# Taking the reciprocal of the decays' running product on GpSimd as a power of -1, from chunk 4 on

## Chip, cores and metric

The kernel runs on one core of a Trainium2 chip. The metric is the device time of one execution in microseconds (us). Two timed executions of the kernel before gave 775.13 and 778.49 us, median 776.81 us. The profile is of a third execution, which took 782.45 us; its span from first to last instruction is 780.6 us, so 1.85 us lie around the span.

Names: PE is the matrix engine (TensorE), PEld its weight loads, DVE is VectorE, ACT is ScalarE, POOL is GpSimd, and SP is the engine whose queue issues most of the DMAs.

## The reference

Two blocks follow each other. The first is a recurrence over 768 time steps for 4 batches and 8 heads with a 40x40 state each; the second is a two-layer feed-forward block on its 3072x320 output.

```python
# recurrence, state (B, H, D, D), B, H, S, D = 4, 8, 768, 40
for t in range(S):
    y[:, :, t] = np.einsum('bhd,bhde->bhe', rt, state)
    Sa = np.einsum('bhde,bhe->bhd', state, at)
    state_decay = state * wt[:, :, None, :] - np.einsum('bhd,bhe->bhde', Sa, bt)
    state = state_decay + np.einsum('bhd,bhe->bhde', vt, kt)
...
x = attn_out.transpose(0, 2, 1, 3).reshape(B * S, H * D)
h = x @ w_in            # 320 -> 2048
g = h * np.cos(h)
return g @ w_out        # 2048 -> 320
```

The decays `w` lie between 0.85 and 0.95.

## The kernel before

The 768 steps are cut into 24 chunks of 32 steps. A chunk has 128 rows (4 batches by 32 steps), so each of its inputs is a tile of 128 partitions by 320 columns (8 heads by 40). Inside a chunk the recurrence is written as small matrix products. For that the decays are multiplied up along the chunk, and `b` and `k` are divided by this running product while `a` is multiplied by it. The division needs the reciprocal of the product, a tile `rw` of 128x320 for every chunk.

From chunk 4 on the running products come from memory: `ws_scan` multiplies them up for four chunks at once, `ws_store` writes them out to `wd`, and `load` reads them back into `nat_w` (two buffers, one for even chunks and one for odd). For chunks 0 to 3 they come out of PSUM (`wn`), which is not touched by the change.

The order of all work is written out by hand in a string, `PLAN`. Each token stands for one step, and the steps are emitted in this order, so every engine and every DMA queue runs its own instructions strictly in that order. The tokens that matter here, with the lines of the profile:

- `r:c` is `over_w` (L453 to L457): the reciprocal `rw` (L455, DVE), then `bn` = `b` times `rw` on POOL (L456).
- `pw:c` is `p1_w`, for two chunks: transposes of `nat_w` on PE, a copy `wb` on ACT (L442), a small copy `wc` (L444) and a memset of the first columns of `wb` to 1 (L451), both on POOL.
- `pa:c` is `p1_a`: transposes of `nat_a` on PE (tile `aps`), then `aT` = `aps` times `wb` on DVE (L461).
- `pb:c` is `p1_b`: transposes of `bn` on PE (tile `bT`, L411) and copies on ACT. `pn:c` multiplies `bT` and `aT` on PE (tile `nps`); ACT copies the result for the inversion, a chain of small DVE steps (`ip`, `ij`; L545 to L576).
- `kn:c` is `p2_kn`: `k` times `rw` on POOL (L631), and a copy of `v` (L632). `in:c` is `p2_in`: copies of `v` and `r` on POOL (L625). `k:c` and `v:c` transpose them on PE (`kT`, `vT`).
- `z:c` is `ch_z`, the state's step: products on PE (tile `dps`), an addition on DVE (L806), the multiplication of the state tile `qz` by the decays on POOL (L807, four instructions), and the output rows `yt` (addition on DVE L813, multiplication on POOL L818). The next chunk starts with `t:c+1`, transposes of `qz` on PE (tile `sT`, L697).
- `tk:c` stores `yt` to DRAM (`xd`, L828, SP queue), `tb:c` reads it back turned as `xT` (L839, L841). `xT` feeds the feed-forward block: `fa`/`fb` (first layer, tile `ph`), `y` (cosine and product on ACT and DVE), `sd` (second layer, tile `po`).
- `ld:c:w` is `load` (L238) of a chunk's `nat_w`, four DMAs on the SP queue. It may overwrite the buffer only once the reciprocal of chunk c-2 has read it.
- `wf`, `wt`, `wg`, `wm`, `wp` (L313 to L340) fetch and convert the feed-forward weights in the first 160 us, mostly on DVE and ACT. `B` and `K` are matrix products without use that keep PE running in the first 150 us.

The inversion is done for four chunks at once. From about 160 us on the feed-forward block of earlier chunks fills PE. In `PLAN`, `r:4` and `r:5` stand on either side of `pw:4`; `r:7`, `r:6` stand before `z:3` with no other POOL work of the state between; `r:9`, `r:8` before `z:4` likewise. Later reciprocals stand singly or in pairs between other steps, as `r:16` before `z:10` and `r:20` before `z:14`.

Of the kernel before, what the change touches and what calls it, by code (L numbers as in the profile page):

```python
# [12 lines left out]
ALU = mybir.AluOpType  # L13
# [92 lines left out]
def kernel(  # L106
# [43 lines left out]
    nc = tc.nc  # L150
    B, H, S, D = r.shape
    P, C, DP = 128, 32, 64
# [23 lines left out]
    def kept(name, shape, n=1, fill=None, part=lambda t: t, on=nc.gpsimd):  # L176

        tiles = []
        for i in range(n):
            t = const.tile(shape, F32, tag=f"{name}{i}", name=f"{name}{i}")  # L180
            if fill is not None:
                on.memset(part(t), fill)
            tiles.append(t)
        return tiles
# [97 lines left out]
    warm = kept("warm", [P, 1])[0]  # L282
    nc.scalar.activation(warm, half_pi, ACTF.Sin)
    rnd = kept("rnd", [P, 1], 1, ROUND)[0]
    bn_b = kept("bn", [P, H, DP], 7, 0.0, padding)
    for i in (4, 5):
        nc.gpsimd.memset(bn_b[i][:, :, C // 2 : C], 0.0)
# [164 lines left out]

    def over_w(c, wn):  # L453
        rw = ring.tile([P, H, D], F32, tag="rw", name="rw")
        nc.vector.reciprocal(rw, wn)  # L455
        nc.gpsimd.tensor_tensor(unpad(bn_b[c % 7]), unpad(nat["b", c]), rw, ALU.mult)  # L456
        G["rw", c] = rw  # L457

# [7 lines left out]
    def p1_a(c):  # L466
        if c >= 4:
            ps = two("aps")
            for i in range(2):
                turned(ps[i], nat["a", c + i])  # L470
            for i in range(2):
                a_W(c + i, ps[i])
            return
        for c in range(c, c + 2):
            wn = ps_h.tile([P, 512], F32, tag="h", name="wn")
            aps = ps_o.tile([P, 512], F32, tag="o", name="aps")
            for j in range(4):
                nc.tensor.transpose(
                    wn[:, j * P : (j + 1) * P], G["wb", c][:, j * P + 1 : (j + 1) * P + 1], ident
                )  # L480
            from_one(c)
            turned(aps, nat["a", c])
            over_w(c, unpad(wn.rearrange("p (h d) -> p h d", h=H)))
            a_W(c, aps)
# [439 lines left out]
    with tc.manual_schedule():  # L924
# [24 lines left out]
        def shifted_(n):  # L949
# [6 lines left out]

        ACTS = {
            "r": lambda c: over_w(c, unpad(nat["w", c])), "lo": lambda c: G["lower", c](), "sp": inv_space,
            "pw": p1_w, "pa": p1_a, "pb": p1_b, "pn": p1_n,
            "L": first_load, "ld": lambda c, n: load(c, n), "la": lambda c, n: load(c, n, nc.scalar),  # L960
# [44 lines left out]
```

## Time and profile before

| | |
|---|---|
| median of two timed runs | 776.81 us (775.13 to 778.49) |
| profiled execution / its span | 782.45 us / 780.6 us |
| PE busy in the span | 742.6 us, 95% |
| DVE busy | 489.7 us, 63% |
| ACT busy | 384.0 us, 49% |
| POOL busy | 188.8 us, 24%, 364 instructions |
| share of PE in the chain that ended last | 89% |
| reciprocals on DVE | 20 from `nat_w`, 42.4 us; 4 from `wn`, 8.6 us |
| first and last start of the 20 | 122.4 and 557.0 us |

Busy time is the time in which an engine has an instruction in execution. The profile also lists, for a group of instructions, how long its engine sat idle before them and which event ended the wait ("<-DVE rw L455" is: released by the reciprocal). PE's busy time is modelled, since matrix products are pipelined. PEclk is the share of its full speed that PE's clock was granted in a stretch. In a timeline each row is start, duration, engine, line and operation, merged where the same instruction is repeated ("x4").

### The profile page before, as it was taken

The numbers are of one execution on the slowest core, as the hardware profiler recorded it, in microseconds if no ns is written. First come the engines' busy times: TensorE is split into PE (matmuls) and PEld (weight loads), VectorE is DVE, ScalarE is ACT, GpSimd is POOL, SyncE is SP. The second block draws the span as 40 slices with busy tenths as digits, with TensorE's granted clock in tenths as the row PEclk, the third lists the DMA queues.
The fourth block names the chain that finished last, engine by engine and source line by source line (L and its number), as shares of the span: only waits on it lengthen the run. The fifth ranks groups of instructions, "written<-read, shape, count | busy, mean of one in ns | idle before, by whom it ended". The sixth has DMA issues, their size and how long they took to land.

```text
span 780.6 us, 39597 instructions
## 1 busy us (share of the span) xinstructions
PE 742.6 (95%) x17812; PEld 577.4 (74%) x17812; DVE 489.7 (63%) x1095; ACT 384.0 (49%) x772; POOL 188.8 (24%) x364
## 2 busy tenths in 40 slices
PE   5687899989999999999999999999999999999997
PEld 4455678777787787778787777777777777777774
DVE  8888889876555886635876746786345883343331
ACT  1435564744455635446545545445455365455352
POOL 7715304301320321221221233022122202210000
PEclk9889899999999999999999999999999999999999
DMA  8655465544424243214423333331302222101000
GB/s 114 159 141 159 129 153 114 101 100 92 81 76 73 46 92 60 54 66 72 72 71 63 55 87 68 52 65 22 78 22 54 39 47 50 36 11 31 19 18 17
DMA packets 176104, 55.79 MB, mean 71 GB/s; under 512 B 149472, under 2 KB 170976, under 8 KB 175936
## 3 DMA queue, kind: packets, MB, share of 16 engines
q1 hardware_dynamic: 173632, 51.54, 31.2%
q8 instruction: 140, 2.29, 1.2%
q0 software_dynamic: 1216, 1.56, 1.2%
q10 hardware_dynamic: 1088, 0.16, 0.1%
q14 instruction: 28, 0.23, 0.1%
HBM read 42.07 MB, written 11.14 MB: 68 GB/s over the span
## 4 chain that ended last, share of the span: by engine, by line
PE 89%; DVE 3%; DMA 2%; issue 2%; POOL 1%; ACT 1%; SPq 1%; DVEq 0%; ACTq 0%; POOLq 0%
PE ph L187 28%; PE po L187 27%; PE dps L187 5%; PE x0ps L187 5%; PE gram L187 4%; PE vT L411 3%; PE sps L187 2%; PE sT L697 2%; PE qps L187 2%; PE nps L187 2%; PE busy L187 2%; PE below L187 1%; PE kT L411 1%; PE bT L411 1%; PE aps L411 1%
## 5 line engine op out<-in xcount | busy, mean ns | idle before, releaser
L187 PE MATMUL po<-w_out_sb,gT 128*128 128x320 f32 x768 | 225.3, 440 | 0.0
L187 PE MATMUL ph<-xT,w_in_sb 128*128 128x256 f32 x768 | 184.7, 387 | 2.4 <-DMA xT<-xd 2.4
L187 PEld LDWEIGHTS po<-w_out_sb,gT 128*128 128x128 f32 x768 | 140.6, 190 | 54.4 <-issue 1.7
L187 PEld LDWEIGHTS ph<-xT,w_in_sb 128*128 128x128 f32 x768 | 142.1, 191 | 34.9 <-issue 12.1
L887 DVE SCALAR_TENSOR_TENSOR turns<-turns,ph 128x512 f32<-128x512 f32 x96 | 64.3, 684 | 115.6 <-ACT turns L885 115.4
L885 ACT ACTIVATE turns<-ph,rnd 128x512 f32<-128x512 f32 x96 | 64.4, 686 | 124.6 <-PE ph L187 123.6
L807 POOL TENSOR_TENSOR qz<-qz,wc 128x160 f32<-128x160 f32 x92 | 40.1, 460 | 210.5 <-DVE qz L806 210.5
L895 DVE TENSOR_TENSOR gT<-ph,turns 128x512 f32<-128x512 f32 x96 | 65.0, 686 | 40.4 <-ACT turns L892 40.3
L892 ACT ACTIVATE turns<-turns,half_pi 128x512 f32<-128x512 f32 x96 | 69.3, 722 | 3.1
L891 ACT ACTIVATE turns<-turns 128x512 f32<-128x512 f32 x96 | 60.0, 625 | 4.7 <-DVE turns L887 4.6
L187 PE MATMUL ph<-xT,w_in_tail 64*64 64x256 f32 (+1 forms) x512 | 54.1, 393 | 0.0
L549 DVE TENSOR_TENSOR inv<-inv,inv_tmp 128x31 f32<-128x31 f32 (+15 forms) x124 | 47.4, 383 | 4.3
L715 ACT COPY qz<-qps 40x256 f32<-40x256 f32 x92 | 33.8, 367 | 30.0 <-PE qps L187 28.1
L545 DVE TENSOR_TENSOR inv_tmp<-u,inv 128x31 f32<-128x31 f32 (+15 forms) x124 | 44.6, 359 | 3.2
L456 POOL TENSOR_TENSOR bn<-nat_b,rw 128x320 f32<-128x320 f32 x22 | 19.7, 899 | 110.6 <-DVE rw L455 46.7
L455 DVE RECIPROCAL rw<-nat_w 128x320 f32<-128x320 f32 x20 | 42.4, 2134 | 0.5 <-DMA nat_w<-wd 0.5
L806 DVE TENSOR_TENSOR qz<-dps,qz 128x160 f32<-128x160 f32 x92 | 29.1, 317 | 21.5 <-PE dps L187 21.3
L187 PEld LDWEIGHTS ph<-xT,w_in_tail 64*64 64x64 f32 (+1 forms) x512 | 31.8, 160 | 8.8 <-issue 4.0
L818 POOL TENSOR_TENSOR yt<-yt,wb 128x512 f32<-128x512 f32 x24 | 31.6, 1316 | 20.5 <-DVE yt L813 20.5
L625 POOL COPY vp<-nat_v 128x320 f32<-128x320 f32 x24 | 11.8, 491 | 93.5 <-DMA nat_v<-in_v_dram 71.1
L759 ACT COPY sm<-sps 128x160 f32<-128x160 f32 x48 | 13.6, 290 | 40.2 <-PE sps L187 33.5
L701 ACT COPY s<-sT 104x416 f32<-104x416 f32 x46 | 21.2, 516 | 23.3 <-PE sT L697 23.2
(138 smaller groups left out, 1096.8 us busy)
## 6 DMA issues: line engine op xcount, KB each, us to landing
words<-in_moe_w_in_dram SPq DMA_DIRECT2D x8, 512.0 KB
xd<-yt SPq DMA_DIRECT2D x48, 80.0 KB
out_dram<-ot SPq DMA_DIRECT2D x24, 160.0 KB
nat_v<-in_v_dram SPq DMA_DIRECT2D x88, 40.0 KB
nat_r<-in_r_dram SPq DMA_DIRECT2D x88, 40.0 KB
nat_k<-in_k_dram SPq DMA_DIRECT2D x88, 40.0 KB
nat_b<-in_b_dram SPq DMA_DIRECT2D x86, 40.0 KB
nat_a<-in_a_dram SPq DMA_DIRECT2D x82, 40.0 KB
```

The source lines that it names most:

```text
L187: nc.tensor.matmul(o, lhsT=lhsT, rhs=rhs, start=start, stop=stop, skip_group_check=True)
L411: nc.tensor.transpose(ps[:, i * P : (i + 1) * P], x[:, 2 * i : 2 * i + 2].rearrange("p e d -> p (e d)"), ident)
L455: nc.vector.reciprocal(rw, wn)
L545: nc.vector.tensor_tensor(tmp, u[:, j : j + 1, :j].to_broadcast([P, C - j, j]), x[:, j:, j : j + 1].to_broadcast([P, C - j, j]), ALU.mult,)
L549: nc.vector.tensor_tensor(x[:, j:, :j], x[:, j:, :j], tmp, ALU.subtract)
L715: nc.scalar.copy(pick(qz[rows], f * (NZ - C), (NZ, 2 * B), (1, C)), ps[f][rows, : 2 * B * C].rearrange("p (i t) -> p i t", t=C),)
L807: nc.gpsimd.tensor_tensor(z, z, wc.rearrange("p (f m b) -> p f m b", f=2, m=2)[:, :, :, bb] .unsqueeze(3).to_broadcast([P, 2, 2, D]), ALU. ...
L885: nc.scalar.activation(t, u, ACTF.Identity, bias=rnd, scale=1.0)
L887: nc.vector.scalar_tensor_tensor(t, t, -ROUND, u, ALU.add, ALU.subtract)
L891: nc.scalar.activation(t, t, ACTF.Abs)
L892: nc.scalar.activation(t, t, ACTF.Sin, bias=half_pi, scale=-2.0 * math.pi)
L895: nc.vector.tensor_tensor(gT[:, 2 * e : 2 * e + 2, :n], phs[e], ns[e].rearrange("p (f t) -> p f t", f=2), ALU.mult)
```

## The change

A constant tile `neg` of 128x1, filled with -1.0 by a POOL memset at the start, is added. In `over_w`, chunks 4 to 23 take `rw` as `nat_w` to the power of `neg` on POOL, where `neg` is read as a second tensor broadcast over 8x40 columns. Chunks 0 to 3 keep DVE's reciprocal, whose input lies in PSUM. The position in `PLAN` stays, so 20 instructions leave DVE's queue and enter POOL's queue, each right in front of its own `bn` multiplication. No other instruction changes its place on any engine. What waited for DVE's reciprocal (the `nat_w` loads on SP) waits for POOL's power instead.

```diff
+    neg = kept("neg", [P, 1], 1, -1.0)[0]
...
     def over_w(c, wn):
         rw = ring.tile([P, H, D], F32, tag="rw", name="rw")
-        nc.vector.reciprocal(rw, wn)
+        if c < 4:
+            nc.vector.reciprocal(rw, wn)
+        else:
+            nc.gpsimd.tensor_tensor(rw, wn, neg.unsqueeze(2).to_broadcast([P, H, D]), ALU.pow)
         nc.gpsimd.tensor_tensor(unpad(bn_b[c % 7]), unpad(nat["b", c]), rw, ALU.mult)
         G["rw", c] = rw
```

## The prediction

> **What bounds the kernel now.** I read the busy shares first, then the costliest groups, the windows of 20 us, and the timelines of POOL, SP and PE around each of the 20 reciprocals. Page, parts 1 and 5:
>
> ```profile
> PE 742.6 (95%) x17812; PEld 577.4 (74%) x17812; DVE 489.7 (63%) x1095; ACT 384.0 (49%) x772; POOL 188.8 (24%) x364
> ...
> L456 POOL TENSOR_TENSOR bn<-nat_b,rw 128x320 f32<-128x320 f32 x22 | 19.7, 899 | 110.6 <-DVE rw L455 46.7
> L455 DVE RECIPROCAL rw<-nat_w 128x320 f32<-128x320 f32 x20 | 42.4, 2134 | 0.5 <-DMA nat_w<-wd 0.5
> ```
>
> PE is the bound. POOL waits 46.7 us for the reciprocals, but it is off the path. The windows (PE, PEld, DVE, ACT, POOL busy, then PEclk) say where PE has holes:
>
> ```profile
> 120.00:140.00 20.00, 19.25 (x419) 15.70 (x407) 19.06 (x35) 10.54 (x20) 8.61 (x15) 1.00 0.61 137
> 140.00:160.00 20.00, 18.94 (x525) 15.44 (x525) 16.30 (x32) 13.88 (x28) 8.79 (x17) 1.00 0.44 78
> 160.00:180.00 20.00, 17.64 (x528) 13.98 (x528) 14.58 (x43) 9.25 (x21) 0.53 (x1) 0.91 0.40 87
> ...
> 220.00:240.00 20.00, 20.00 (x546) 16.52 (x546) 6.74 (x19) 9.72 (x22) 5.62 (x13) 1.00 0.34 91
> ```
>
> From 120 us on PE is idle 0.75 + 1.06 + 2.36 + 0.61 us to 200 us, and some 0.5 us later up to 760. So even perfect relief gains at most about 5 us, 0.7%. The 42.4 us leave an engine that is not the bound. What counts is what the power does to POOL's queue. POOL's timeline at the first three pairs of reciprocals:
>
> ```profile
> 122.78 1.27 POOL L818 TENSOR_TENSOR yt<-yt,wb 128x512 f32<-128x512 f32 x1
> 124.67 1.13 POOL L456 TENSOR_TENSOR bn<-nat_b,rw 128x320 f32<-128x320 f32 x1 [0.62 <-ACT wb L442]
> ...
> 143.35 0.13 POOL L451 MEMSET wb<- 128x16 f32 x1
> 147.11 1.69 POOL L456 TENSOR_TENSOR bn<-nat_b,rw 128x320 f32<-128x320 f32 x2 [3.64 <-DMA nat_b<-in_b_dram]
> 149.76 1.75 POOL L807 TENSOR_TENSOR qz<-qz,wc 128x160 f32<-128x160 f32 x4 [0.96 <-DVE qz L806]
> 151.47 1.27 POOL L818 TENSOR_TENSOR yt<-yt,wb 128x512 f32<-128x512 f32 x1
> ...
> 193.35 0.45 POOL L625 COPY rp<-nat_r 128x320 f32<-128x320 f32 x1
> 193.76 1.68 POOL L456 TENSOR_TENSOR bn<-nat_b,rw 128x320 f32<-128x320 f32 x2
> 195.40 1.71 POOL L807 TENSOR_TENSOR qz<-qz,wc 128x160 f32<-128x160 f32 x4
> ```
>
> The second and third pair stand right in front of the state's multiplication L807. PE's rows that need this work, and SP's:
>
> ```profile
> 132.65 1.09 PE L411 MATMUL bT<-ident,bn 128*128 128x128 f32 x8
> ...
> 163.26 2.89 PE L187 MATMUL ph<-xT,w_in_sb 128*128 128x256 f32 x8 [2.36 <-DMA xT<-xd]
> ...
> 197.37 0.89 PE L697 MATMUL sT<-ident,qz 104*104 104x104 f32 x8
> ```
>
> ```profile
> 127.20 2.99 SPq L238 DMA_DIRECT2D nat_w<-wd  x4
> ...
> 155.56 2.40 SPq L828 DMA_DIRECT2D xd<-yt  x2
> ```
>
> The transposes sT start 0.3 us after the last L807 ends (197.1). PE's one long wait, at 163.26, is for xT, which hangs on the store xd at 155.56.
>
> **The change, part by part.** Removed from DVE: 20 x 2.134 = 42.7 us. It ends no wait of PE that I can find, so I put it at 0; its bound is the 5 us above. The new memset of `neg` is one of POOL's 128x1 fills, 0.1 us at 3 us, while POOL's DMA issues run until 12 us: 0.
>
> Added to POOL: 20 powers of X us each. No row has a power. Below, the nearest row is POOL's multiplication of the same shape, 0.86 us. For arithmetic that is more than a pass I have only DVE: a plain two-input step of 128x160 takes 317 ns (L806), one of 128x512 682 ns (L461, median), so 320 columns would take 0.48 us; the reciprocal takes 2.13, 4.4 times that. POOL's 0.86 times 4.4 is 3.8 us, the price of one such function. A power with its exponent in a tensor is a logarithm, a product and an exponential: 3.8 + 0.86 + 3.8 = 8.5 us, an estimate, and the value I take. As the upper end I put two dozen steps at 0.86 us, 20 us. Both ends stay for the range.
>
> The Trainium skill speaks against the move as such: the GPSIMD Engine Reference, section 4.1, sends elementwise arithmetic to VectorE, about twice as fast for two inputs. The trace agrees in kind, 0.86 against 0.48. Its section 3.1 puts two-input work on GpSimd down to the read port and not to arithmetic; by that alone X would be 0.86.
>
> First place, chunks 4 to 7. POOL is free at 124.1. The power, bn, two wc and two memsets (1.5 us together) and the second power end at 125.6 + 2X. SP's nat_w load at 127.20 is chunk 7's, which waits for chunk 5's reciprocal (it ended at 127.14): it moves by 2X - 1.5. SP's queue is back to back from there to 158 us, so everything behind moves too, nat_b for chunk 7 among it, on which POOL waits until 147.1. The order there is power 7 (hidden in that wait), bn, power 6, bn, so these end at 147.1 + (2X - 1.5) + 0.86 + X + 0.86 = 147.3 + 3X. Behind them queue L807 (1.75) and L818 (1.25): yt is ready at 150.3 + 3X, and xd, now 155.56, starts then or when SP's own delay lets it. The wait at 163.26 has no slack, so PE is late by the larger of 2X - 1.5 and 3X - 5.3 (which takes over at 3.8). At 8.5: 20.2 us. PE's earlier stalls, at bT 132.65 (bn ready at 126.5 + 2X: 10 us) and at the next bT at 151 (3X - 3.5: 22.0), lie inside the same 20.2, as the wait at 163 and the holes before it, some 3 us, give that part back. DVE's aT L461 waits too, for the memsets behind power 4: 125.3 + X against 127.05, 6.7 us, with the weight conversion queued behind it; inside the 20.2.
>
> Second place, chunks 9 and 8. The two powers stand between rp (ends 193.8) and L807 (starts 195.40), and POOL can't start them earlier, because vp before them waits for its DMA until 192.96. L807 moves by 2X, sT's slack is 0.3: 2X - 0.3, at 8.5 16.7 us. SP's nat_w loads for chunks 11 and 10 (190.25 on) wait as long; the next xd, 10.6 us behind its yt, absorbs that.
>
> The clock: after the wait of 2.36 us at 163.26, the windows 163 to 167 and 167 to 171 show a granted clock of 0.64 and 0.93, so 1.44 + 0.28 = 1.7 us are lost to it. Two long stalls that end on the path: 3.4 us. The Trainium skill (TensorE: Matmul & The Clock Gate, Part 1) says the same in a rule: half clock after about one idle window of 3.4 us, full again after one busy window. The trace's half clock came after a wait shorter than that.
>
> The other 12 powers, by POOL's room until the step that needs it: chunks 10 and 11 stall PE only from X = 13 (203.8 + 2X against sT's limit 230), 12 and 13 from 9 (265.3 + 2X against 283.3), 14 and 15 from 13, the six single ones (16, 17, 20 to 23) from 13 (chunk 23) to 25 (chunk 16). Chunks 18 and 19 hold up wb, and so DVE's aT at 447.2, from X = 6.4: 2X - 12.8 = 4.2 us of DVE, of which PE may see none or all; I take half, 2.1.
>
> Sum at 8.5: 20.2 + 16.7 + 3.4 + 2.1 = 42.4 us. On the profiled execution 782.45 + 42.4 = 824.9; on the median, 5.6 us lower, 776.8 + 42.4 = 819.
>
> **Rivals.**
> *The power is as cheap as a pass* (not slower). If POOL's loop hides the arithmetic behind reading its two inputs, X is 0.86: 0.2 + 1.4 us, no clock loss, 778 us. For it: POOL's copy of one input takes 0.45 and its product of two 0.86, so reading counts. Against: DVE's own function costs 4.4 passes. Below 3.5 (5.5 + 6.7 + 3.4 = 15.6 us) the change stays within 2% (15.5 us), about what a measurement of this kernel can tell from no change; that is the point from which the case decides. Chance of X under 3.5: 0.25, of which 0.05 lie under 1.3.
>
> *POOL becomes the bound.* If the power runs in a loop that is not vectorised well, X is over 20. At 20: 54.7 + 39.7 + 3.4, then 13.7 (10, 11), 22 (12, 13), 13.9 (14, 15), 17.6 (18, 19) and 10 for the rest: 175 us, 952 us. Beyond it each us of X costs up to 20. For it: no row limits it; against: POOL's other elementwise groups all take under 1.4 us. Chance 0.17.
>
> The Trainium skill's GPSIMD Engine Reference, section 7, gives 4 cycles an element to each link of a dependent chain; at its 1.2 GHz, 320 elements are 1.07 us a link, an estimate, so 8 links would give 8.5 us and 19 would give 20.
>
> *Relief wins.* A gain over 2% needs 15.5 us and there are 5 to win: 0.01.
>
> **How the numbers follow.** Forecast (X from 3.5 to 20): 0.57. Range: X = 1.3 gives 1.1 + 2.3 = 3.4 us, 780; X = 20 gives 952. Outside lie 0.05 below and 0.17 above, with the 0.01 of a gain. Slower by over 2%: 0.57 + 0.17 = 0.74; within 2%: 0.25; faster: 0.01. The forecast case's own range is 792 to 952.
>
> **What would show it.** The group of powers on POOL with its mean; PE waits at sT of chunk 4 near 2X; xd of chunk 3 late by 3X - 5.3; the nat_w load of chunk 7 issued at the end of power 5; DVE 42.7 us less busy without a shorter span; half-clock stretches behind the stalls. A power under 3.5 us makes the forecast wrong by its size; POOL starting the powers long before their old place would make it wrong by mechanism.

## The result, and the profile after

| | before | after |
|---|---|---|
| median of two timed runs | 776.81 us | 1663.24 us (1661.03 to 1665.46) |
| ratio after to before, 95% interval | | 2.141 [2.118, 2.165] |
| span of the profiled execution | 780.6 us | 1659.3 us |
| mean granted clock of PE in it | 0.983 | 0.727 |

The change makes the kernel 886 us slower. The forecast was 819 us with a range of 780 to 952, so the time lies far outside it, on the side of the second rival. Page of the kernel after, from parts 1, 2, 4 and 5:

```profile
PE 779.7 (47%) x17812; PEld 599.8 (36%) x17812; DVE 450.7 (27%) x1075; ACT 386.9 (23%) x772; POOL 1213.4 (73%) x385
...
PE   5891140072025058019306093800807446199998
...
POOL 7239989948999948995994949699399697922110
PEclk9895575586558579559657587855858677699999
...
POOL 56%; PE 20%; issue 10%; SPq 3%; DMA 3%; DVE 2%; ACT 1%; POOLq 0%; DVEq 0%; ACTq 0%
...
L459 POOL TENSOR_TENSOR rw<-nat_w,neg 128x320 f32<-128x320 f32 x20 | 1026.6, 51332 | 40.8 <-DMA nat_w<-wd 40.6
```

The last line holds the result: a power takes 51.3 us, 60 times POOL's multiplication of the same shape (0.86 us), where the forecast had 8.5 and the upper end 20. The 20 of them are 1026.6 us, more than the whole span of before. POOL's busy time grew by 1024.6 us, from 188.8 to 1213.4; PE's work is the same 17,812 products, but PE is busy for 47% of the span instead of 95%. In part 2 PE and POOL take turns: in 14 of the 20 slices where POOL shows 9, PE shows 0 or 1. The chain that ended last is 56% POOL, where it was 89% PE. DVE is 39.0 us less busy, and nothing came of it.

What PE waits for, in the kernel after (us in total, times, longest):

```profile
PE bT L412 <- POOL bn L460: 284.7, 6, 94.7
PE sT L701 <- POOL qz L811: 257.0, 5, 101.4
PE dps L187 <- DVE aT L465: 87.9, 1, 87.9
PE vT L412 <- POOL vp L629: 84.3, 2, 83.2
PE bT L412 <- DVE aT L465: 79.2, 1, 79.2
PE x0ps L187 <- DVE aT L465: 47.0, 2, 46.8
```

These 17 waits are 840 of the 879 us by which the span grew. They name five different steps, but each stands behind a power in POOL's queue: `bn`, the state's multiplication (L811, L807 before), the copies for `vT`, and the memset that `aT` waits for. Fifteen of them are longer than 20 us; the other two are 0.15 and 1.02 us. Most of the other 39 us is the clock: PE is busy 37.1 us longer for the same products (779.7 against 742.6), and 15 long stalls at the 2.2 us that the run with four powers measures for one would be 33 us, an estimate.

POOL's timeline of the kernel after, at the powers of chunks 4 to 7, with some instructions between them left out:

```profile
122.80 51.36 POOL L459 TENSOR_TENSOR rw<-nat_w,neg 128x320 f32<-128x320 f32 x1
...
175.78 51.32 POOL L459 TENSOR_TENSOR rw<-nat_w,neg 128x320 f32<-128x320 f32 x1
...
236.02 0.20 POOL L445 COPY wc<-wb 128x16 f32<-128x16 f32 x1 [5.98 <-ACT wb L443]
...
237.09 51.31 POOL L459 TENSOR_TENSOR rw<-nat_w,neg 128x320 f32<-128x320 f32 x1
288.49 0.86 POOL L460 TENSOR_TENSOR bn<-nat_b,rw 128x320 f32<-128x320 f32 x1
289.30 51.31 POOL L459 TENSOR_TENSOR rw<-nat_w,neg 128x320 f32<-128x320 f32 x1
340.69 0.86 POOL L460 TENSOR_TENSOR bn<-nat_b,rw 128x320 f32<-128x320 f32 x1
341.51 1.71 POOL L811 TENSOR_TENSOR qz<-qz,wc 128x160 f32<-128x160 f32 x4
343.18 1.27 POOL L822 TENSOR_TENSOR yt<-yt,wb 128x512 f32<-128x512 f32 x1
```

PE's rows behind them:

```profile
176.20 0.44 PE L187 MATMUL x0ps<-vvm,ag 32*32 32x72 f32 x2 [46.85 <-DVE aT L465]
...
228.09 1.11 PE L412 MATMUL bT<-ident,bn 128*128 128x128 f32 x4 [46.74 <-POOL bn L460]
...
341.61 1.97 PE L412 MATMUL bT<-ident,bn 128*128 128x128 f32 x8 [94.69 <-POOL bn L460]
```

And SP's:

```profile
227.13 1.79 SPq L238 DMA_DIRECT2D nat_w<-wd  x4
...
344.48 0.70 SPq L832 DMA_DIRECT2D xd<-yt  x2
```

The order is, but for one step, the one that the prediction walked through. The first power holds up the memset for `aT`, and PE with it, for 46.85 us. The load of chunk 7's `nat_w` is issued when power 5 ends (175.78 + 51.32 = 227.10; the row starts at 227.13). The last two powers stand in front of L811, then `yt`, then the store `xd`, which moved from 155.56 to 344.48. The step that differs is power 7 (the third here): no wait for `nat_b` hides it here; POOL's only idle time shortly before it is the 5.98 us in front of `wc`. The part on why the prediction was wrong comes back to it.

### The profile page after: what moved, and what is told of

It is laid out like the page before. It is cut to its first block, busy times and chain, and to the rows that moved or that the text cites. A ratio compares the mean times of both kernels' runs of the same rounds, so it can differ in the third digit from the quotient of the medians.

```text
span 1659.3 us, 39571 instructions
## 1 busy us (share of the span) xinstructions
PE 779.7 (47%) x17812; PEld 599.8 (36%) x17812; DVE 450.7 (27%) x1075; ACT 386.9 (23%) x772; POOL 1213.4 (73%) x385
## 4 chain that ended last, share of the span: by engine, by line
POOL 56%; PE 20%; issue 10%; SPq 3%; DMA 3%; DVE 2%; ACT 1%; POOLq 0%; DVEq 0%; ACTq 0%
POOL rw L459 53%; PE ph L187 7%; PE po L187 7%; SPq L238 3%; PE x0ps L187 1%; POOL qz L811 1%; PE gram L187 1%; PE dps L187 1%; DMA nat_w<-wd 1%; PE sT L701 1%; POOL bn L460 1%; PE vT L412 1%; POOL yt L822 1%; PE qps L187 1%; PE sps L187 0%
## 5 line engine op out<-in xcount | busy, mean ns | idle before, releaser
L459 POOL TENSOR_TENSOR rw<-nat_w,neg 128x320 f32<-128x320 f32 x20 | 1026.6, 51332 | 40.8 <-DMA nat_w<-wd 40.6
L412 PE MATMUL bT<-ident,bn 128*128 128x128 f32 x96 | 19.9, 364 | 363.9 <-POOL bn L460 284.7
L811 POOL TENSOR_TENSOR qz<-qz,wc 128x160 f32<-128x160 f32 x92 | 40.7, 469 | 154.2 <-DVE qz L810 154.1
L701 PE MATMUL sT<-ident,qz 104*104 104x104 f32 x184 | 28.9, 314 | 257.0 <-POOL qz L811 257.0
L465 DVE TENSOR_TENSOR aT<-aps,wb 128x512 f32<-128x512 f32 x24 | 15.6, 682 | 491.1 <-POOL wb L452 304.9
L412 PEld LDWEIGHTS bT<-ident,bn 128*128 128x128 f32 x96 | 15.4, 188 | 367.5 <-POOL bn L460 286.7
L701 PEld LDWEIGHTS sT<-ident,qz 104*104 104x104 f32 x184 | 22.6, 160 | 261.8 <-POOL qz L811 260.9
L496 ACT COPY bT<-bT 128x512 f32<-128x512 f32 x24 | 13.7, 588 | 298.0 <-PE bT L412 297.9
L187 PE MATMUL dps<-vvm,kn 32*64 32x72 f32 (+1 forms) x1536 | 24.1, 237 | 90.1 <-DVE aT L465 87.9
L412 PE MATMUL vT<-ident,vp 128*128 128x128 f32 x96 | 17.3, 310 | 84.3 <-POOL vp L629 84.3
L187 PEld LDWEIGHTS dps<-vvm,kn 32*64 32x64 f32 (+1 forms) x1536 | 20.3, 130 | 97.9 <-DVE aT L465 88.4
```

Of the source, the lines that this page charges most:

```text
L187: nc.tensor.matmul(o, lhsT=lhsT, rhs=rhs, start=start, stop=stop, skip_group_check=True)
L412: nc.tensor.transpose(ps[:, i * P : (i + 1) * P], x[:, 2 * i : 2 * i + 2].rearrange("p e d -> p (e d)"), ident)
L459: nc.gpsimd.tensor_tensor(rw, wn, neg.unsqueeze(2).to_broadcast([P, H, D]), ALU.pow)
L701: nc.tensor.transpose(ps[i // 4][:n, (i % 4) * n : (i % 4 + 1) * n], qz[:n, i // 2, i % 2, C : C + n], ident[:n, :n])
L811: nc.gpsimd.tensor_tensor(z, z, wc.rearrange("p (f m b) -> p f m b", f=2, m=2)[:, :, :, bb] .unsqueeze(3).to_broadcast([P, 2, 2, D]), ALU. ...
```

## The experiments

Two questions were open. First, is it the duration of the power alone, or does the new place in POOL's queue cost something, or does DVE's relief bring something? Second, how does the loss grow with that duration, and why by more than the prediction's sum would give? All edits are to the kernel after, unless said otherwise. The kernel before was run beside them: 779.21 us median (774.93 to 782.43) for the first four, 772.96 us (769.54 to 777.97) for the last two.

### One multiplication in the power's place

```diff
-nc.gpsimd.tensor_tensor(rw, wn, neg..., ALU.pow)
+nc.gpsimd.tensor_tensor(rw, wn, neg..., ALU.mult)
```

`rw` becomes the negative product instead of its reciprocal.

> Chunks 4 to 23 multiply nat_w by -1 on GpSimd in the place of the power, so rw is the negative product and not its reciprocal; DVE's 20 reciprocals stay away, order as in the changed kernel. Theory (the loss is the power's duration alone; the move itself and DVE's relief are worth nothing): X is 0.86, the prediction's sums give 0.2 + 1.4 us, so 775 to 780 us beside 777. Rival A (freeing 42.7 us of DVE is worth something once the power is cheap): 772 or less, at most 5 us down. Rival B (a longer POOL queue, or DVE and POOL in each other's way, costs by itself): over 785 us, and POOL's other groups longer than before.

Measured: 778.32 us (774.80 to 782.34), ratio 0.9994 [0.9967, 1.0021]. Page, parts 1 and 5:

```profile
PE 742.8 (95%) x17812; PEld 575.9 (74%) x17812; DVE 457.2 (59%) x1075; ACT 384.4 (49%) x772; POOL 204.9 (26%) x385
...
L459 POOL TENSOR_TENSOR rw<-nat_w,neg 128x320 f32<-128x320 f32 x20 | 14.6, 732 | 42.8 <-DMA nat_w<-wd 42.6
```

The instruction has the power's place, operands and waits, takes 0.73 us, and costs nothing. POOL's other work is no longer than before (`qz` takes 460 ns in both), so the two engines are not in each other's way here. So the whole loss is the power's duration. DVE is relieved as in the kernel after, and that is worth nothing that 0.3% could show: the prediction's zero for it stands, and there is no gain to fetch by moving the reciprocal off DVE.

### Ten multiplications, and four

After the one multiplication, nine more (or three more) of `rw` by `neg`, each dependent on the one before it: a power of about 7.9 us (or 3.1 us). `rw` is then the product with a sign. In one thing this stand-in differs from a power: only the first multiplication reads `nat_w`. SP issued the load of chunk 7 at 130.11 here, when the first multiplication of the second "power" had ended (129.36 + 0.72), and not when its tenth had (138.6). So the delay of that load, 2X - 1.5 in the prediction's first place, is shorter here than a power of the same length would make it: by some 7 us with ten multiplications, by 2.4 us with four.

```diff
+for _ in range(9):
+    nc.gpsimd.tensor_tensor(rw, rw, neg..., ALU.mult)
```

> As the single multiplication, but ten in a row on the same tile, 8 to 9 us for each reciprocal that left DVE; rw is then not the reciprocal. This gives X the size that the prediction assumed. Theory (its path through the queue was right and only X was off): +42 us, 812 to 828 us, with a wait of about 2X at sT of chunk 4 and xT of chunk 3 late by about 3X - 5.3. Rival A (every us on POOL costs nearly as much as in the changed kernel, 886 us for 1027 us of powers): 20 x 8.5 x 0.86 = 146 us, 923 us. Rival B (waits hidden behind the feed-forward work): under 790 us.

Measured: 836.97 us (834.29 to 844.42), ratio 1.0766 [1.0718, 1.0814], or 58 us more. The expectation of 812 to 828 was missed. To see where, the start of the transposes `sT` of each chunk is set against that in the kernel before; the growth of this lag from one chunk to the next is the cost of a place. The first two places (chunks 4 to 7, then 9 and 8) cost 17.6 and 15.3 us, where the prediction's formulas give 18.4 and 15.5 at 7.9 us. The first agreement is luck. POOL at the third and fourth "power" (chunks 7 and 6):

```profile
148.73 0.21 POOL L445 COPY wc<-wb 128x16 f32<-128x16 f32 x1 [6.34 <-ACT wb L443]
...
149.81 0.72 POOL L459 TENSOR_TENSOR rw<-nat_w,neg 128x320 f32<-128x320 f32 x1
...
157.86 0.93 POOL L462 TENSOR_TENSOR bn<-nat_b,rw 128x320 f32<-128x320 f32 x1
158.74 0.72 POOL L459 TENSOR_TENSOR rw<-nat_w,neg 128x320 f32<-128x320 f32 x1
```

The formula hides the third behind a wait for `nat_b`. Here it starts behind `wc`, which waited 6.34 us for ACT's `wb`, and the `bn` after it waits for no load. All four stand in line. With the load released that early the prediction's formula would give 2X - 4.6, or 11.2 us, and not 17.6.

The later places, for which the prediction has nothing at this size but 1.5 us (chunks 18 and 19) and 3.4 us of clock, cost 26.3 us. One of them, in POOL's timeline (chunk 16):

```profile
398.29 0.72 POOL L459 TENSOR_TENSOR rw<-nat_w,neg 128x320 f32<-128x320 f32 x1 [20.83 <-DMA nat_w<-wd]
...
406.26 0.85 POOL L462 TENSOR_TENSOR bn<-nat_b,rw 128x320 f32<-128x320 f32 x1
407.08 1.72 POOL L813 TENSOR_TENSOR qz<-qz,wc 128x160 f32<-128x160 f32 x4
```

POOL is idle for 20.83 us in front of the power, but this time can't be used, because `nat_w` isn't there. The prediction counted it as room. What the same place looked like in the kernel before, in POOL's and in SP's timeline:

```profile
365.26 0.86 POOL L456 TENSOR_TENSOR bn<-nat_b,rw 128x320 f32<-128x320 f32 x1 [25.00 <-DVE rw L455]
366.08 1.71 POOL L807 TENSOR_TENSOR qz<-qz,wc 128x160 f32<-128x160 f32 x4
```

```profile
356.70 5.61 SPq L238 DMA_DIRECT2D nat_w<-wd  x8
```

POOL's idle time there is 25.00 us, the room that the prediction gave to chunk 16. The row names DVE's reciprocal as what ended it, and hides that the reciprocal's input was loaded only from 356.70 on. When it had landed is shown by POOL's timeline of the kernel with one multiplication at the same place (that kernel runs some 2 us ahead of before there):

```profile
360.92 0.72 POOL L459 TENSOR_TENSOR rw<-nat_w,neg 128x320 f32<-128x320 f32 x1 [22.58 <-DMA nat_w<-wd]
...
363.41 1.75 POOL L811 TENSOR_TENSOR qz<-qz,wc 128x160 f32<-128x160 f32 x4 [0.82 <-DVE qz L810]
```

The step starts when the load has landed, 2.5 us before the state's multiplication: there are a few us of room, not 25. The run with four powers measures them.

The smaller one:

> Four multiplications in a row in the place of the power, some 3.2 us for each; rw is not the reciprocal. It stands near the point from which the prediction let the case decide (3.5 us, +15.6 us). Theory: (2 x 3.2 - 1.5) + (2 x 3.2 - 0.3) + half clock of 0 to 3.4 us, and next to nothing from later places: +11 to +15 us, 788 to 796 us. Rival A (in proportion to the ten multiplications): 58 x 3.2 / 7.9 = 23 us, 802 us. Rival B (nothing until POOL's room is used up): 776 to 781 us.

Measured: 786.38 us (785.33 to 790.0), ratio 1.0153 [1.0089, 1.0218], or 13.4 us more. The difference is the 11 to 15 us expected (the absolute time is lower because the kernel before ran at 772.96 us on that chip). The parts fit less well: the first place costs 1.2 us instead of 4.7, the second 4.8 instead of 5.9, and places that should cost nothing (chunks 10 and 11, chunk 22) cost 2.1 and 2.2 (all read from one profile of each kernel). At the first place the early release explains a part: with it the formula gives 3.1 + 0.7 - 1.5 = 2.3 us, not 4.7. So the total fits partly by luck, with errors of both signs that cancel.

### The power at four places alone

```diff
-if c < 4:
+if c not in (8, 9, 16, 20):
```

> The power for chunks 8, 9, 16 and 20 only; the other chunks keep DVE's reciprocal. Theory (a power costs what its place leaves uncovered): chunks 9 and 8 stop PE at sT of chunk 4 for 2 x 51.3 - 0.3 = 102 us, chunk 16 holds the state's multiplication of chunk 10 by 340.3 + 52.2 - 366.1 = 26 us, chunk 20 that of chunk 14 by 462.3 + 52.2 - 482.9 = 32 us; with some 5 us of half clock +165 us, 942 us. Rival (POOL's throughput is the bound, so each power costs its length): +205 us, 982 us, with equal waits of 51 us behind 16 and 20.

Measured: 981.43 us (980.63 to 982.24), ratio 1.2606 [1.2552, 1.2661]; 202 us more, which is the rival's 982 and not the theory's 942. PE's timeline right behind the state's steps of chunks 4 and 10:

```profile
295.78 1.84 PE L701 MATMUL sT<-ident,qz 104*104 104x104 f32 x8 [101.58 <-POOL qz L811]
...
514.34 1.84 PE L701 MATMUL sT<-ident,qz 104*104 104x104 f32 x8 [45.84 <-POOL qz L811]
```

POOL's, in front of the powers of chunks 16 and 20:

```profile
461.61 51.32 POOL L459 TENSOR_TENSOR rw<-nat_w,neg 128x320 f32<-128x320 f32 x1 [20.73 <-DMA nat_w<-wd]
...
628.19 51.32 POOL L459 TENSOR_TENSOR rw<-nat_w,neg 128x320 f32<-128x320 f32 x1 [15.41 <-DMA nat_w<-wd]
```

The pair 9, 8 makes one wait of 101.58 us, as 2X - 0.3 says (102.3). The single powers cost waits of 45.84 and 45.82 us, so they have some 5.5 us of room and not 13 to 25: both had to wait for their `nat_w` (20.73 and 15.41 us) with POOL idle. That is neither theory's wait exactly: the rival, no room at all, would have 51, and its total fits because the two missing times of 5.5 us are nearly made up by the three waits' cost in clock and by lags of a few us elsewhere.

The same run prices the clock by itself. Windows behind the wait of 101.58 us (PE, PEld, DVE, ACT, POOL busy, PEclk, DMA share, GB/s):

```profile
298.00:300.00 2.00, 2.00 (x10) 1.82 (x9) 0.00 (x0) 1.34 (x3) 1.42 (x3) 0.50 0.53 82
300.00:304.00 4.00, 4.00 (x89) 2.90 (x88) 0.00 (x0) 1.22 (x4) 0.00 (x0) 0.88 0.53 103
304.00:310.00 6.00, 6.00 (x207) 4.45 (x206) 3.54 (x4) 3.42 (x7) 0.00 (x0) 1.00 0.35 55
```

PE runs at half clock from the wait's end until about 301 (0.96 us of the second window at 0.50 make its 0.88), then at full. The lag grows by 2.2 us there and no further. By the granted clock, the way in which the prediction came to 1.7 us for the stall of 2.36 us in the kernel before, it would be 2.6 us (5.2 us at half). Either way a stall some 40 times as long costs at most about 1 us more of clock. The rule of the Trainium skill (TensorE: Matmul & The Clock Gate, Part 1) that one busy window of about 3.4 us brings the full clock back fits these rows: the page calls the window free-running, so a stall may end in the middle of one, and PE was at half clock for some 5 us here (295.78 to 301). The mean clock of 0.727 in the kernel after is therefore a sign of 15 long stalls, and not what cost most of the time.

### Half of the heads

DVE takes the reciprocal of four heads, POOL the power of the other four.

```diff
+nc.vector.reciprocal(rw[:, HH:], wn[:, HH:])
+nc.gpsimd.tensor_tensor(rw[:, :HH], wn[:, :HH], neg..., ALU.pow)
```

> From chunk 4 on the power takes four of the eight heads (160 columns), DVE's reciprocal the other four; the product is the reference's. Price of a power by the run that measured it alone: 0.38 + 160 x 0.157 = 25.5 us. Theory now (the path through the queue as predicted for chunks 4 to 9, but the later powers find hardly any room, since nat_w lands just before its old place): on the line between the ten multiplications (7.9 us, +58) and the changed kernel (51.3 us, +884), +395 us, 1150 to 1195 us. Rival A (the rooms of the prediction hold for chunks 10 to 23): its sums at 25.5 give +275 us, 1052 us. Rival B (POOL's throughput alone, 0.86 us for each us of power as in the changed kernel): 20 x 25.5 x 0.86 = 439 us, 1218 us.

Measured: 1151.06 us (1149.43 to 1152.69), ratio 1.4869 [1.4745, 1.4992], or 378 us more: inside the 1150 to 1195 of the theory, and not the 1052 or 1218 of the others. Page, part 5:

```profile
L460 POOL TENSOR_TENSOR rw<-nat_w,neg 128x160 f32<-128x160 f32 x20 | 516.9, 25844 | 42.1 <-DMA nat_w<-wd 41.9
```

Half of the columns take half of the time, 25.84 us. Between this run and the kernel after, the loss grows by (886 - 378) / (51.33 - 25.84) = 19.9 us for each us of X. There are 20 powers, so every one lies on the path in full. Both runs lie on the line 20X - 139 us: a power has 6.9 us of room on average, and no more. The line is for long powers alone: at 7.9 us it would give 19 us, and 58 were measured.

### The power by itself

The kernel before, with seven short instructions on POOL after its last step, where nothing waits for them: one multiplication and six powers, on a `nat_w` tile. Not shown is the helper `timed`, which issues one instruction.

```diff
...
+timed(ALU.mult, 32, neg)        # columns, exponent
+timed(ALU.pow, 32, neg)
+timed(ALU.pow, 16, neg)
+timed(ALU.pow, 32, half_pi)     # exponent 1.57
+timed(ALU.pow, 32, neg, 8)      # 8 partitions
+timed(ALU.pow, 24, neg, first=x[:, D:])    # padding, all 1.0
+nc.gpsimd.tensor_tensor(probe[:, n : n + 32], x[:, :32], x[:, :32], ALU.pow)
```

> The kernel before, with seven instructions added at the end of POOL's queue, after its last yt, writing to a tile that nobody reads: a multiplication of 32 columns, powers of -1 of 32 and of 16 columns, a power of 1.57 (32 columns), a power of -1 on 8 partitions (32 columns), a power of -1 of 24 columns that all hold 1.0, and a power of 32 columns with a full second tensor. Theory (a fixed price per column, whatever the values): 160 ns a column, so 5.1, 2.6, 5.1, 5.1, 3.9 and 5.1 us, the 8 partitions too at 5.1 if a core works its 16 partitions side by side, 2.6 if one after another. Rival A (the exponent -1 or the broadcast makes it slow): the power of 1.57 or the full second tensor is far shorter. Rival B (the time hangs on the values): the columns of 1.0 are far shorter. The whole ends some 30 us after 725 us, before PE does: 775 to 780 us.

Measured (775.22 us for the whole, one run): groups at the end of the span, each shape apart, in the columns of part 5. The first group holds the multiplication (0.24 us) and the power of the same shape (5.46 us).

```profile
L986 POOL TENSOR_TENSOR probe<-nat_w,neg 128x32 f32<-128x32 f32 x2 | 5.7, 2847 | 0.0
...
L986 POOL TENSOR_TENSOR probe<-nat_w,neg 8x32 f32<-8x32 f32 x1 | 5.4, 5405 | 0.0
L986 POOL TENSOR_TENSOR probe<-nat_w,half_pi 128x32 f32<-128x32 f32 x1 | 5.4, 5403 | 0.0
L994 POOL TENSOR_TENSOR probe<-nat_w 128x32 f32<-128x32 f32 x1 | 5.4, 5403 | 0.0
...
L986 POOL TENSOR_TENSOR probe<-nat_w,neg 128x24 f32<-128x24 f32 x1 | 4.1, 4143 | 0.0
...
L986 POOL TENSOR_TENSOR probe<-nat_w,neg 128x16 f32<-128x16 f32 x1 | 2.9, 2890 | 0.0
```

From 16 to 32 columns a power grows by 2.51 us, so 157 ns a column and 0.38 us around it; 320 columns give 50.6 us, and 51.3 was measured. Eight partitions take as long as 128, an exponent of 1.57 as long as -1 (5.40 us), a full second tensor as long as a broadcast column, and for 24 columns of 1.0 the line gives 4.15 and 4.14 was measured. So among the things varied here the price goes by columns alone; neither these data nor the way in which the exponent is read makes it. What POOL does in these 157 ns no run here shows.

## Why the prediction was wrong

**The step that failed** is the size of X, the time of one power. The prediction took 0.86 us times 4.4, DVE's ratio of a reciprocal to a plain step, for a logarithm and again for an exponential, and came to 8.5 us, with an upper end of "two dozen steps at 0.86 us, 20 us". Measured are 51.3 us. How one engine's reciprocal stands to its plain step said nothing about another engine's power, and the upper end was a count of steps that no row bears out. The Trainium skill's GPSIMD Engine Reference, section 3.1, gives the read port as the floor of two-input work. For this operation the floor is far off: a multiplication and a power read the same operands, and for 32 columns they took 0.24 and 5.46 us. Nor do the 8 or 19 dependent links that the prediction reckoned with from section 7 of the same page of the Trainium skill, at an estimated 1.07 us each, reach the measured time.

**The case that occurred** is the rival "POOL becomes the bound", at a chance of 0.17. That POOL then bounds the kernel is what the waits of the kernel after show; whether the power runs "in a loop that is not vectorised well", as that rival supposed, no run shows. Its price of 175 us at X = 20 was too low: the line through the two large runs gives 20 x 20 - 139 = 261 there, an estimate; "beyond it each us of X costs up to 20" was right (19.9).

**The path, place by place.** The prediction's formulas with the measured X put in, against the growth of the lag of `sT` in the kernel after:

| place | formula | at 51.3 us | measured |
|---|---|---|---|
| chunks 4 to 7 | 3X - 5.3 | 148.6 | 189.4 |
| chunks 9, 8 | 2X - 0.3 | 102.3 | 100.9 |
| chunks 10, 11 | 2X - 26 | 76.6 | 82.4 |
| chunks 12, 13 | 2X - 18 | 84.6 | 84.5 |
| chunks 14, 15 | 2X - 26 | 76.6 | 81.9 |
| chunk 16 | X - 25 | 26.3 | 52.1 |
| chunks 18, 19 | 2X - 22.4, from its 17.6 at 20 | 80.2 | 92.0 |
| chunk 23 | X - 13 | 38.3 | 41.9 |
| chunks 17, 20, 21, 22 | X - 25 to X - 13 | 105 to 153 | 155.5 |

With the right X the sum would have been 739 to 787 us, clock left aside, of the 880 measured; the sign and most of the size follow from X alone. Two places make up much of the rest.

- *First place.* The formula hides power 7 in POOL's wait for `nat_b`. In the kernel after, PE had by then stopped twice (46.85 and 46.74 us), so the transposes `pw:6` and ACT's `wb` behind them were late. POOL waited 5.98 us for that copy, and power 7 started at 237.09, after all of the wait in which it was to hide. All four powers then lie on the path: between the half-heads run (87.7 us here, X = 25.84) and the kernel after (189.4) this place grows by 3.99 us for each us of X. From ten multiplications (17.6 at 7.9 us) to half of the heads it already grows by 3.9. So the order in the formula did not hold there either, and 18.4 against 17.6 was luck. In the two large runs, where real powers hold `nat_w` to their ends, no `bn` of this place waits for `nat_b`.
- *Rooms of later places.* They were read from POOL's idle time in front of `bn`. The four-places run showed 5.5 us at chunks 16 and 20, where 13 to 25 stood, because the power can't start before its `nat_w` has landed. The other later places were not tried alone; that the same holds there is argued from their sum.

**What was right.** DVE's relief at nothing (0.9994 with one multiplication, DVE 39.0 us less busy after, against 42.7); the new place in the queue at nothing; `nat_w` of chunk 7 issued at the end of power 5; the waits at `sT` of chunk 4 near 2X; the clock at about 2 us for a long stall, though with 15 of them instead of two. POOL started no power long before its old place.

## What to carry to other kernels

An operation that no row of a profile has on its engine could not be sized here from another engine's ratio; time it by itself first, in a few instructions at the kernel's end with two widths, before a kernel is built on it. Before idle time in front of an instruction is counted as room, follow its operands back to the load that they come from: a wait that is put down to the producer may have been the producer's own wait. A long instruction in an in-order queue costs nearly its whole length (45.8 of 51.3 us here) once it stands in front of the one step that every chunk must pass.

## What was not expected of the hardware

- A power of two f32 tensors on POOL takes 157 ns for each column, on 8 partitions as on 128, the same for every base and exponent tried, and 51.3 us for 128x320; DVE's reciprocal of that shape takes 2.13 us.
- POOL's multiplication of 128x320 by one broadcast column takes 0.73 us, against 0.86 us for `bn`, which reads two full tensors and whose tiles are laid out with gaps.
- After a stall of PE of 101.6 us, the half clock cost 2.2 us by the lag and 2.6 us by the granted clock; after one of 2.36 us it cost 1.7 us by the granted clock.
